# A state-space layer beside a gated feed-forward: state projection first, B transposed on TensorE, small angle tables, a fixed VectorE order

## The chip, the cores and the metric

The kernel runs on one core of a Trainium2 chip. The metric is the device time of one execution in microseconds. Before the change it is 227.94 us, the median of three runs (227.24, 227.94 and 227.97).

## The reference

The input x has 2048 rows of 512 numbers (bf16). Each row is normalised (xn). Two branches read xn:

- A diagonal state-space layer with 512 complex states: `h[t] = Lam_bar * h[t-1] + B_bar @ xn[t]`, with `Lam_bar = exp(dt * Lam)` and `B_bar = ((Lam_bar - 1) / Lam) * B`, and the output `s = 2 * Re(C @ h) + xn * Dskip`.
- A gated feed-forward of width 1376: `g = silu((gelu(xn @ w_gate) * (xn @ w_up)) @ w_down)`.

The result is `x + s * g`.

## The kernel before, in words

The 2048 rows are worked in four slabs (s = 0 to 3) of 512 rows. Columns of states and of the model are cut into tiles of 128: four for the states (pt), four for the model (kt), eleven for the feed-forward (j, the last with 96).

Per slab there are four kinds of TensorE work. `u_pair` (line 272) projects xn on the states, in two halves (h) of 16 matmuls; ScalarE evicts each group of four to `U`. `ffn` (324) makes one of eleven gate and up tiles (`g_ps`, `up_ps`); ScalarE evicts them as `gt` (with Gelu) and `ub`, and VectorE multiplies them to `at`. `down` (345) is 11 matmuls for 128 rows, four times a slab; ScalarE takes a Tanh of it and VectorE combines both to `g2`. `y_mm` (362) is the output projection of 128 rows from the states `hst` and the folded matrix `C2`; `epi` (378) multiplies with `g2`, adds x, and stores. PSUM has four buffers for `u_ps`, `g_ps` and `up_ps` together, two for `f_ps` and two for `y_ps`; `gt` and `ub` have four each.

`chain` (297) is the recurrence, on VectorE alone. The complex factor is split into its size `rho` and its angle: `rotate` (287) turns `U` by the tables of cosine and sine, real scans of 512 steps (four for a half of the states) run with `rho`, the last value is turned on for the next slab, and a second `rotate` gives `hst`. One half is 3.5 us of products, four scans, and 3.5 us of products.

Slab 0 has the order: eleven `ffn` tiles, with `fold_c` (254, C times the coefficients of B_bar, two ScalarE passes and two VectorE operations per state tile) after tiles 3 to 6; then the two state projections with their chains; then the norms of slabs 2 and 3; then `down`. Slabs 1 to 3 have the projections first, then the `ffn` tiles, and after tiles 4, 6, 8 and 10 an output projection of the slab before. The output projections of slab 3 come at the end.

What stands ahead of the loop: B and C are loaded by eight transposing DMAs each (lines 90 to 92 and 208 to 210); the weights are issued from ScalarE's queue, all else from SyncE's. `ln_stats` (132) and `ln_norm` (145) do the norms on VectorE, with the inverse root as a power on GpSimd; slab 0 is transposed on TensorE, the others by DMA (`ln_dma`, 153). The tables of 512 angles for four state tiles are made in full: VectorE multiplies and reduces the angles (lines 175 to 191), ScalarE takes the sine and the cosine (194, 195).

TensorE, ScalarE, SyncE and GpSimd run in the order written. VectorE does so only up to line 251; after it, a scheduler orders VectorE by priorities, with `at`, `g2` and the epilogue ahead of the chains (`tc.high_priority`).

Of the kernel before, what the change touches and what calls it, by code (L numbers as in the profile page):

```python
# [19 lines left out]
def kernel(  # L20
# [84 lines left out]
    halfpi = consts.tile([P, 1], FP32, name="halfpi")
    nc.vector.memset(halfpi[:], math.pi / 2)


    pt_ps = ps_y.tile([P, 16], BF16, name="pt_ps", tag="y")
    nc.tensor.transpose(pt_ps[:, :], pv[:, :], ident[0:16, 0:16])  # L110
    pf = consts.tile([P, 16], FP32, name="pf")
    nc.vector.tensor_copy(out=pf[:], in_=pt_ps[:, :])
    lre, lim, ldt, dsk = (pf[:, 4 * i : 4 * i + 4] for i in range(4))

    def small(name, w=NPT):
        return consts.tile([P, w], FP32, name=name)

    dt_ = small("dt_")
    nc.scalar.activation(out=dt_[:], in_=ldt, func=AF.Exp)
    a1 = small("a1")  # L120
    nc.vector.tensor_tensor(out=a1[:], in0=lre, in1=dt_[:], op=ALU.mult)
    thn = small("thn")
    nc.vector.scalar_tensor_tensor(
        out=thn[:], in0=lim, scalar=1.0 / (2.0 * math.pi), in1=dt_[:], op0=ALU.mult, op1=ALU.mult
    )
    rho = small("rho")
    nc.scalar.activation(out=rho[:], in_=a1[:], func=AF.Exp)


    xn_t = {}  # L130

    def ln_stats(s):
        st = work.tile([P, M, 6], FP32, name="st", tag="st")
        mv = consts.tile([P, M, 2], FP32, name=f"mv{s}")
        for m in range(M):
            nc.vector.bn_stats(out=st[:, m, :], in_=x_tok[:, s * M + m, :])  # L136
        for m in range(M):
            nc.vector.bn_aggr(out=mv[:, m, :], in_=st[:, m, :])
        ve = work.tile([P, M], FP32, name="ve", tag="ve")
        nc.vector.tensor_scalar(out=ve[:], in0=mv[:, :, 1], scalar1=EPS, scalar2=None, op0=ALU.add)  # L140
        rs = consts.tile([P, M], FP32, name=f"rs{s}")
        nc.gpsimd.tensor_tensor(out=rs[:], in0=ve[:], in1=mhalf[:], op=ALU.pow)  # L142
        return mv, rs

    def ln_norm(s, m, mv, rs):
        xn = work.tile([P, D], BF16, name="xn", tag="xn", bufs=4)
        nc.vector.tensor_scalar(  # L147
            out=xn[:], in0=x_tok[:, s * M + m, :], scalar1=mv[:, m, 0:1], scalar2=rs[:, m : m + 1],
            op0=ALU.subtract, op1=ALU.mult,
        )  # L150
        return xn

    def ln_dma(s):
        with tc.high_priority():
            mv, rs = ln_stats(s)
            xs = [ln_norm(s, m, mv, rs) for m in range(M)]
        for m in range(M):
            c0 = s * TS + m * P
            nc.sync.dma_start_transpose(out=xnT[:, :, c0 : c0 + P], in_=xs[m][:])

    mv, rs = ln_stats(0)
    xs = [ln_norm(0, m, mv, rs) for m in range(M)]
    for m in range(M):
        tp = ps_f.tile([P, KT, P], BF16, name="tp", tag="f")
        for kt in range(KT):
            nc.tensor.transpose(tp[:, kt, :], xs[m][:, kt * P : (kt + 1) * P], ident[:])  # L166
        nc.vector.tensor_copy(out=xnT[:, :, m * P : (m + 1) * P], in_=tp[:, :, :])


    cos_b = consts.tile([P, NPT, TS], BF16, name="cos_b")  # L170
    sinp = consts.tile([P, 2, NPT, TS], BF16, name="sinp")
    W2 = TS + 2
    ang = work.tile([P, NPT, W2], FP32, name="ang", tag="hst")
    angk = work.tile([P, NPT, W2], FP32, name="angk", tag="hst")
    for pt in range(NPT):
        nc.vector.tensor_scalar(
            out=ang[:, pt, :], in0=iota_f[:], scalar1=thn[:, pt : pt + 1], scalar2=None, op0=ALU.mult
        )
        nc.vector.tensor_scalar(
            out=angk[:, pt, :], in0=iota_f[:], scalar1=thn[:, pt : pt + 1], scalar2=MAGIC,  # L180
            op0=ALU.mult, op1=ALU.add,
        )

    nr = ang
    nc.vector.scalar_tensor_tensor(
        out=nr[:], in0=angk[:], scalar=MAGIC, in1=ang[:], op0=ALU.subtract, op1=ALU.subtract
    )
    ab = angk
    nc.vector.scalar_tensor_tensor(
        out=ab[:], in0=nr[:], scalar=-1.0, in1=nr[:], op0=ALU.mult, op1=ALU.max  # L190
    )
    cs = consts.tile([P, 2, NPT], FP32, name="cs")
    sn = consts.tile([P, 2, NPT], FP32, name="sn")
    nc.scalar.activation(out=sinp[:, 1, :, :], in_=nr[:, :, 0:TS], func=AF.Sin, scale=-TWO_PI)
    nc.scalar.activation(out=cos_b[:], in_=ab[:, :, 0:TS], func=AF.Sin, scale=-TWO_PI, bias=halfpi[:])
    for i, c in enumerate((1, TS)):
        nc.scalar.activation(out=sn[:, i, :], in_=nr[:, :, c], func=AF.Sin, scale=-TWO_PI)
        nc.scalar.activation(out=cs[:, i, :], in_=ab[:, :, c], func=AF.Sin, scale=-TWO_PI, bias=halfpi[:])
# [251 lines left out]
```

## Time and profile before

| | us |
|---|---|
| median of three runs | 227.94 |
| profiled execution | 225.93 |
| its span, first to last instruction | 224.2 |
| TensorE matmuls busy | 183.6 (82%) |
| VectorE busy | 173.4 (77%) |
| ScalarE busy | 95.1 (42%) |
| GpSimd busy | 6.4 (3%) |
| mean granted TensorE clock | 0.952 of full |

The profile is one execution. PE is TensorE, DVE VectorE, ACT ScalarE, POOL GpSimd, SP SyncE; a q behind a name is that engine's queue. L350 is line 350 of the kernel. Busy time counts instructions that overlap at their ends only once in a stretch, while the duration of one instruction is from its start to its end, so operations that follow each other start closer than they last.

### The profile page before, as it was taken

To read this page: it belongs to the slowest core of one execution; us is meant where nothing else is said; L and a number is where in the kernel's file an instruction comes from. 1 tells how busy PE (TensorE), PEld (TensorE's weight loads), DVE (VectorE), ACT (ScalarE), POOL (GpSimd) and SP (SyncE) were. 2 spreads that over 40 slices of the span, in tenths; PEclk is the share of its full clock that TensorE was granted. 3 is DMA by queue.
4 is the path that set the end of the run, shared out by engine and by line. 5 is a ranking of instruction groups with operands and counts; after the bars stand their busy time and mean duration, and the time that the engine had idled before them with its cause. 6 is when DMAs were issued, how large, how long until landed. Compare 5 with 4: busy or idle time off the path is not lost.

```text
span 224.2 us, 2436 instructions
## 1 busy us (share of the span) xinstructions
PE 183.6 (82%) x849; PEld 84.6 (38%) x865; DVE 173.4 (77%) x315; ACT 95.1 (42%) x156; POOL 6.4 (3%) x13
## 2 busy tenths in 40 slices
PE   0018939069966999999829999999999999999993
PEld 0013414024422444445303444444444444454441
DVE  1079869966899899999994279999932999995443
ACT  0221898177620466444201476444225764440310
POOL 3010000140000000000000000000000000000000
PEclk9999988769996999999967999999999999999998
DMA  6998992035510000000000000000100000001001
GB/s 189 327 230 176 341 183 60 0 50 97 107 32 0 0 3 0 0 1 23 26 23 23 0 0 3 0 23 0 47 26 1 0 0 0 26 24 49 23 5 68
DMA packets 24317, 12.26 MB, mean 55 GB/s; under 512 B 15760, under 2 KB 24304, under 8 KB 24304
## 3 DMA queue, kind: packets, MB, share of 16 engines
q1 hardware_dynamic: 21136, 9.28, 17.1%
q10 hardware_dynamic: 3168, 2.82, 4.8%
q8 instruction: 7, 0.11, 0.2%
q14 instruction: 6, 0.05, 0.1%
HBM read 6.33 MB, written 2.10 MB: 38 GB/s over the span
## 4 chain that ended last, share of the span: by engine, by line
PE 49%; DVE 36%; DMA 8%; ACT 4%; POOL 1%; issue 1%; SPq 0%; DVEq 0%; POOLq 0%
PE f_ps L350 13%; PE g_ps L330 10%; PE up_ps L335 9%; PE y_ps L367 9%; DVE Ft L306 8%; PE u_ps L280 6%; DVE st L136 4%; DVE pp L292 4%; DVE qq L293 4%; DMA xnT<-xn 4%; DVE at L343 3%; DMA wu<-in_B_w_up_dram 2%; DMA pv<-in_A_log_dt_dram 2%; DVE xn L147 2%; PE y_ps L372 1%; POOL rs L142 1%
## 5 line engine op out<-in xcount | busy, mean ns | idle before, releaser
L330 PE MATMUL g_ps<-xnT,wg 128*128 128x512 bf16 (+1 forms) x173 | 47.4, 396 | 8.1 <-ACT gt L339 7.4
L350 PE MATMUL f_ps<-wd,at 128*128 128x512 bf16 (+1 forms) x173 | 42.8, 405 | 8.9 <-DVE at L343 5.0
L335 PE MATMUL up_ps<-xnT,wu 128*128 128x512 bf16 (+1 forms) x174 | 46.8, 391 | 3.5 <-ACT ub L341 3.4
L339 ACT ACTIVATE gt<-g_ps 128x512 bf16<-128x512 f32 (+1 forms) x44 | 26.3, 597 | 33.8 <-PE g_ps L330 33.4
L341 ACT ACTIVATE ub<-up_ps 128x512 bf16<-128x512 f32 (+1 forms) x44 | 26.3, 598 | 11.8 <-PE up_ps L335 11.4
L354 ACT ACTIVATE th<-f_ps 128x512 f32<-128x512 f32 x16 | 9.6, 599 | 49.0 <-PE f_ps L350 41.7
L350 PEld LDWEIGHTS <-at 128*128 128x128 bf16 (+1 forms) x176 | 17.9, 103 | 32.3 <-issue 8.8
L367 PE MATMUL y_ps<-C,hst 128*128 128x512 bf16 x124 | 29.9, 379 | 0.2
L306 DVE TENSOR_TENSOR_SCAN Ft<-rho,it,Wt 128x512 bf16<-128x512 f32 x24 | 29.6, 1273 | 0.0
L330 PEld LDWEIGHTS <-wg 128*128 128x128 bf16 (+1 forms) x176 | 17.7, 103 | 28.3 <-issue 11.7
L280 PE MATMUL u_ps<-xnT,BT 128*128 128x512 bf16 x124 | 28.1, 379 | 0.2
L335 PEld LDWEIGHTS <-wu 128*128 128x128 bf16 (+1 forms) x176 | 18.2, 103 | 25.6 <-issue 6.5
L357 DVE SCALAR_TENSOR_TENSOR g<-th,f_ps 128x512 f32<-128x512 f32 x16 | 11.0, 686 | 19.1 <-ACT th L354 19.1
L284 ACT ACTIVATE U<-u_ps 128x512 bf16<-128x512 f32 x32 | 19.1, 598 | 8.2 <-PE u_ps L280 8.2
L280 PEld LDWEIGHTS <-BT 128*128 128x128 bf16 x128 | 12.5, 98 | 15.1
L343 DVE TENSOR_TENSOR at<-gt,ub 128x512 bf16<-128x512 bf16 (+1 forms) x44 | 18.0, 416 | 0.0
L367 PEld LDWEIGHTS <-hst 128*128 128x128 bf16 x128 | 12.4, 98 | 14.3
L292 DVE TENSOR_TENSOR pp<-U,cos_b 128x2048 bf16<-128x2048 bf16 x8 | 9.8, 1222 | 5.7 <-ACT U L284 5.5
L382 DVE TENSOR_TENSOR yg<-y_ps,g 128x512 bf16<-128x512 f32 x16 | 11.0, 686 | 2.3 <-PE y_ps L372 2.2
L166 PE MATMUL tp<-ident,xn 128*128 128x128 bf16 x16 | 2.0, 308 | 10.3 <-DVE xn L147 10.0
L147 DVE TENSOR_SCALAR xn<-x_tok,mv,rs 128x512 bf16<-128x512 bf16 x16 | 6.0, 411 | 5.5 <-DMA xnT<-xn 4.3
L136 DVE BATCH_NORM_STATS2 st<-x_tok 128x6 f32<-128x512 bf16 x16 | 10.1, 684 | 0.0
(74 smaller groups left out, 130.6 us busy)
## 6 DMA issues: line engine op xcount, KB each, us to landing
out_dram<-ot SPq DMA_DIRECT2D x16, 128.0 KB, 1.7
x_tok<-in_A_x_dram SPq DMA_DIRECT2D x3, 512.0 KB, 5.2
wd<-in_B_w_down_dram SPq DMA_DIRECT2D x1, 1280.0 KB
wg<-in_B_w_gate_dram ACTq DMA_DIRECT2D x1, 512.0 KB, 6.1
x_tok<-in_A_x_dram SPq DMA_DIRECT2D x4, 128.0 KB, 4.7
wu<-in_B_w_up_dram ACTq DMA_DIRECT2D x1, 512.0 KB
wg<-in_B_w_gate_dram ACTq DMA_DIRECT2D x1, 480.0 KB
wu<-in_B_w_up_dram ACTq DMA_DIRECT2D x1, 480.0 KB
```

What stands on the lines that cost most here:

```text
L136: nc.vector.bn_stats(out=st[:, m, :], in_=x_tok[:, s * M + m, :])
L280: nc.tensor.matmul(u_ps[:, :], lhsT=BT[:, ri, kt, pt * P : (pt + 1) * P], rhs=xnT[:, kt, cols], start=(kt == 0), stop=(kt == KT - 1),)
L284: nc.scalar.activation(out=U[:, ri, q, :], in_=u_ps[:, :], func=AF.Copy)
L292: nc.vector.tensor_tensor(out=pp[:], in0=src[:], in1=cb, op=ALU.mult)
L306: nc.vector.tensor_tensor_scan(out=Ft[:, ri, q, :], data0=rho[:, pt : pt + 1].to_broadcast([P, TS]), data1=Wt[:, ri, q, :], initial=init, ...
L330: nc.tensor.matmul(g_ps[:fs, :], lhsT=wg[:, kt, fsl], rhs=xnT[:, kt, cols], start=(kt == 0), stop=(kt == KT - 1))
L335: nc.tensor.matmul(u_ps[:fs, :], lhsT=wu[:, kt, fsl], rhs=xnT[:, kt, cols], start=(kt == 0), stop=(kt == KT - 1))
L339: nc.scalar.activation(out=gt[:fs], in_=g_ps[:fs, :], func=AF.Gelu_apprx_tanh)
L341: nc.scalar.activation(out=ub[:fs], in_=u_ps[:fs, :], func=AF.Copy)
L343: nc.vector.tensor_tensor(out=at[:fs, j, :], in0=gt[:fs], in1=ub[:fs], op=ALU.mult)
L350: nc.tensor.matmul(f_ps[:, :], lhsT=at[:fs, k, m0 : m0 + P], rhs=wd[:fs, k, :], start=(k == 0), stop=(k == NFT - 1))
L367: nc.tensor.matmul(y_ps[:, :], lhsT=hst[:, j // NPT, j % NPT, m0 : m0 + P], rhs=C2[:, j // NPT, j % NPT, :], start=(j == 0), stop=False,)
```

## The change

The state projection and the chains of slab 0 now come ahead of its `ffn` tiles. B is loaded as it lies and transposed by 32 matmuls. The angle tables are made by adding angles: sine and cosine of 49 columns (angles 0 to 31, and multiples of 32 up to 512), two broadcast copies on GpSimd, and six VectorE products and sums. The norms of slabs 2 and 3 are taken by ScalarE (two passes with a running sum, seven small GpSimd operations, a third ScalarE pass that normalises); slab 1 keeps its statistics on VectorE and is normalised on ScalarE. The inverse root of slab 0 is Exp(-0.5 Ln) on ScalarE. The weights and C move to SyncE's queue, `fold_c` to the down projections of slab 0, and C's tile shares the two buffers of `hst`. VectorE now runs in the order written, too; `later`, `dve`, `drain` and `flush` write it by two clocks that the code counts for itself.

```diff
-    for ri, src in enumerate((A_B_re, A_B_im)):
-        for kt in range(KT):
-            nc.sync.dma_start(out=BT[:, ri, kt, :], in_=src[:, kt * P : (kt + 1) * P], transpose=True)
+    for ri, src in enumerate((A_B_re, A_B_im)):
+        nc.scalar.dma_start(out=Bn[:, ri, :, :], in_=src.rearrange("(k p) d -> p k d", p=P))
...
+    ACT(out=tiny[:], in_=eps_t[:], func=AF.Ln)
+    def b_transposes(ri):
+        for k0 in range(0, KT, 2):
+            tb = ps_mm.tile([P, 2, D], BF16, name="tb_ps", tag="mm")
+            for k in range(2):
+                for pt in range(NPT):
+                    nc.tensor.transpose(
+                        tb[:, k, pt * P : (pt + 1) * P], Bn[:, ri, pt, (k0 + k) * P : (k0 + k + 1) * P], ident[:]
+                    )
+            ACT(out=BT[:, ri, k0 : k0 + 2, :], in_=tb[:, :, :], func=AF.Copy)
...
+    def rstd_act(s, a, b):
+        ACT(out=lnv[:, a:b], in_=mv[:, s, a:b, 1], func=AF.Ln, bias=eps_t[:])
+        ACT(out=rs[:, s, a:b], in_=lnv[:, a:b], func=AF.Exp, scale=-0.5)
...
+    dummies(6)
+    b_transposes(0)
...
+    rstd_act(0, 0, 2)
+    ACT(out=dt_[:], in_=ldt, func=AF.Exp)
+    b_transposes(1)
+    bn(0, 2)
...
+    rstd_act(0, 2, 4)
...
+    ACT(out=sb[:], in_=ang[:], func=AF.Sin, scale=TWO_PI)
+    ACT(out=cb[:], in_=kr[:], func=AF.Sin, scale=-TWO_PI, bias=halfpi[:])
+    nc.vector.tensor_copy(out=sh[:], in_=sb[:])
+    nc.vector.tensor_copy(out=ch[:], in_=cb[:])
+    nc.gpsimd.tensor_copy(out=v4(ca[:]), in_=ch[:, :, NB : NB + NA].unsqueeze(3).to_broadcast(W4))
+    nc.gpsimd.tensor_copy(out=v4(sa[:]), in_=sh[:, :, NB : NB + NA].unsqueeze(3).to_broadcast(W4))
...
+    def pe_takes(n, one=0.2157):
+        clk["pe"] += n * one
+    def pop():
+        r, c, f, _ = waiting.pop(0)
+        clk["dve"] = max(clk["dve"], r) + c
+        f()
+    def flush(key):
+        while any(w[3] == key for w in waiting):
+            pop()
+    def drain(t):
+        while waiting and max(clk["dve"], waiting[0][0]) + waiting[0][1] <= t + 1.0:
+            pop()
+    def dve(ready, cost, f):
+        drain(ready)
+        clk["dve"] = max(clk["dve"], ready) + cost
+        f()
+    def later(ready, cost, f, key=None):
+        waiting.append((ready, cost, f, key))
...
+        dve(now() + 0.9, 0.34, lambda: TT(out=at[:fs, j, :], in0=gt[:fs], in1=ub[:fs], op=ALU.mult))
...
+    def ln_act(s, m):
+        for i, f in enumerate((AF.Copy, AF.Square)):
+            junk = work.tile([P, D], BF16, name="junk", tag="junk", bufs=1)
+            ACT(out=junk[:], in_=x_tok[:, s * M + m, :], func=f, accum_out=sx[:, s, i, m : m + 1])
...
+    clk["pe"] = 10.0
+    clk["dve"] = 10.0
+    later(10.0, 1.2, lambda: TT(out=v4(t1_[:]), in0=v4(ca[:]), in1=cB, op=ALU.mult))
+    later(10.0, 1.2, lambda: TT(out=v4(t2_[:]), in0=v4(sa[:]), in1=sB, op=ALU.mult))
+    later(10.0, 1.2, lambda: TT(out=cos_b[:], in0=t1_[:], in1=t2_[:], op=ALU.subtract))
...
+    for h in range(2):
+        chain(0, h, u_pair(0, h), hst0)
...
+    dve(17.0, 2.8, ln1_stats)
...
+        for j in range(NFT):
+            ffn(s, j, ats[s])
+            if s == 0:
+                if j == 1:
+                    dve(now(), 2.6, coefficients)
+                if 3 <= j < 3 + M:
+                    ln_out(1, j - 3)
+            else:
+                if s < NS - 1:
+                    if j < M:
+                        ln_act(s + 1, j)
+                    if j == M:
+                        ln_small(s + 1)
+                    if 6 <= j < 6 + M:
+                        ln_out(s + 1, j - 6)
...
         if s < NS - 1:
             for m in range(M):
                 g2s[s, m] = down(s, m, ats[s])
+                if s == 0:
+                    fold_c(m)
```

`chain` and `rotate` hand their operations to `later`, `y_mm` calls `flush` for the states that it reads, and `ln_out` is a ScalarE pass with scale and shift and a transposing DMA.

## Rows read from the trace of the kernel before

**Rows 1.** Busy time by stretch: length, then each engine's busy us, clock, DMA, GB/s

```profile
0.00:18.60 18.60, 2.21 (x17) 1.83 (x18) 6.71 (x23) 2.98 (x4) 2.90 (x10) 1.00 1.01 247
18.65:22.60 3.95, 3.95 (x12) 1.47 (x12) 3.92 (x9) 1.20 (x2) 0.00 (x0) 1.00 0.64 160
60.30:75.40 15.10, 11.31 (x45) 4.73 (x45) 14.37 (x20) 2.40 (x4) 0.00 (x0) 0.89 0.11 21
82.30:116.70 34.40, 29.33 (x144) 13.72 (x145) 34.16 (x57) 13.75 (x23) 0.00 (x0) 0.96 0.04 12
126.00:169.20 43.20, 42.99 (x210) 20.23 (x213) 34.64 (x55) 20.33 (x34) 0.00 (x0) 1.00 0.04 13
169.20:220.30 51.10, 50.84 (x256) 24.23 (x259) 38.08 (x54) 20.94 (x35) 0.00 (x0) 1.00 0.05 16
```

**Rows 2.** Waits from 0 to 60 us: total us, times, longest

```profile
PE g_ps L330 <- ACT gt L339: 7.4, 3, 6.3
PE up_ps L335 <- ACT ub L341: 3.4, 1, 3.4
```

**Rows 3.** Waits from 60 to 117 us

```profile
PE f_ps L350 <- DVE at L343: 5.0, 2, 4.1
PE f_ps L350 <- DVE g L357: 3.7, 1, 3.7
```

**Rows 4.** The chain of waits that ended last: start, length, what

```profile
57.70 0.66 DVE C L259
...
60.01 1.14 DVE pp L292
...
63.60 4.49 DVE Ft L306 x4
...
159.81 9.51 PE f_ps L350 x44
...
176.23 0.86 PE g_ps L330 x4
...
220.38 0.70 DVE yg L382
```

**Rows 5.** All engines in order of time, 0 to 62 us

```profile
15.36 1.38 DVE L147 TENSOR_SCALAR xn<-x_tok,mv,rs 128x512 bf16<-128x512 bf16 x4 [1.22 <-POOL rs L142]
15.82 1.04 PE L166 MATMUL tp<-ident,xn 128*128 128x128 bf16 x8 [10.04 <-DVE xn L147]
...
18.65 1.87 PE L330 MATMUL g_ps<-xnT,wg 128*128 128x512 bf16 x4 [0.51 <-DVE xnT L167]
...
21.77 1.03 PE L330 MATMUL g_ps<-xnT,wg 128*128 128x512 bf16 x4
```

**Rows 6.** ScalarE in order of time, 30 to 36 us

```profile
30.19 0.19 ACT L197 ACTIVATE sn<-ang 128x4 f32<-128x4 f32 x1
...
33.15 0.59 ACT L341 ACTIVATE ub<-up_ps 128x512 bf16<-128x512 f32 x1
33.62 0.72 ACT L257 ACTIVATE tA<-CT,cim 128x512 f32<-128x512 bf16 x1
34.24 0.72 ACT L258 ACTIVATE tB<-CT,cim 128x512 f32<-128x512 bf16 x1
```

**Rows 7.** ScalarE in order of time, 9 to 32 us: start, length, what

```profile
11.45 1.28 ACT L339 ACT_TABLE_LOAD   x1
20.55 0.60 ACT L339 ACTIVATE gt<-g_ps 128x512 bf16<-128x512 f32 x1 [7.82 <-PE g_ps L330]
26.47 1.91 ACT L194 ACTIVATE sinp<-ang 128x2048 bf16<-128x2048 f32 x1
```

**Rows 8.** GpSimd's groups by form: busy us, mean ns of one, idle before

```profile
L142 POOL TENSOR_TENSOR rs<-ve,mhalf 128x4 f32<-128x4 f32 x4 | 4.6, 1157 | 40.3 <-DVE ve L140 40.3
L100 POOL CAST iota_f<-iota_i 128x514 f32<-128x514 int32 x1 | 0.6, 614 | 0.1
...
masks.py:199 POOL TENSOR_SCALAR_AFFINE_SELECT ident_f<-ident_f 128x128 f32<-128x128 f32 x1 | 0.3, 293 | 0.1
...
L102 POOL MEMSET mhalf<- 128x4 f32 x1 | 0.1, 102 | 0.0
```

More of the change, by code (lines that the diff above doesn't have):

```diff
@@ L44 @@
     NPT = 4
+    H2 = NPT // 2
     TS = 512
@@ L105 @@
[L105 to L198, printed above, removed]
@@ L207 @@
     nc.sync.dma_start(out=wd[:FL, NFT - 1, :], in_=B_w_down[(NFT - 1) * P : F, :])
[L208 to L216 removed]
+    warm = consts.tile([P, TS], BF16, name="warm")
+    nc.vector.memset(warm[:], 0.0)
+    halfpi = consts.tile([P, 1], FP32, name="halfpi")
@@ new lines, with small, dummies @@
+    iota_f = consts.tile([P, NBA], FP32, name="iota_f")
+    nc.gpsimd.tensor_copy(out=iota_f[:], in_=iota_i[:])
+    mhalf = consts.tile([P, M], FP32, name="mhalf")
+    nc.gpsimd.memset(mhalf[:], -0.5)
+    tiny = consts.tile([P, 1], FP32, name="tiny")
+    ACT(out=tiny[:], in_=eps_t[:], func=AF.Ln)
+    def small(name, w=NPT):
+        return consts.tile([P, w], FP32, name=name)
+    def dummies(n):
+        w_ps = ps_f.tile([P, TS], FP32, name="w_ps", tag="f")
+        for _ in range(n):
+            nc.tensor.matmul(w_ps[:, :], lhsT=warm[:, 0:P], rhs=warm[:], start=True, stop=True)
@@ new lines @@
+    rho = small("rho")
+    ACT(out=rho[:], in_=a1[:], func=AF.Exp)
+    for m in range(2, 4):
+        tp = t_xn0(m, xs[m])
+        nc.vector.tensor_copy(out=xnT[:, :, m * P : (m + 1) * P], in_=tp[:, :, :])
+    W3 = [P, NPT, NBA]
+    ang = consts.tile(W3, FP32, name="ang")
+    kr = consts.tile(W3, FP32, name="kr")
+    sb = consts.tile(W3, FP32, name="sb")
+    cb = consts.tile(W3, FP32, name="cb")
+    sh = consts.tile(W3, BF16, name="sh")
+    ch = consts.tile(W3, BF16, name="ch")
+    TT(out=ang[:], in0=iota_f[:].unsqueeze(1).to_broadcast(W3), in1=thn[:].unsqueeze(2).to_broadcast(W3), op=ALU.mult)
@@ L297, in chain, with wt, wt_dst @@
     def chain(s, h, U, hst):
         hs = slice(h * H2, (h + 1) * H2)
-        Wt = work.tile([P, 2, H2, TS], BF16, name="Wt", tag="Wt")
-        rotate(Wt[:, 0, :, :], Wt[:, 1, :, :], U, h, ALU.add)
-        Ft = work.tile([P, 2, H2, TS], BF16, name="Ft", tag="Ft")
+        ready = now() + 0.9
+        box = {}
+        def wt():
+            box["W"] = work.tile([P, 2, H2, TS], BF16, name="Wt", tag="Wt", bufs=1)
+            return [box["W"][:, i, :, :] for i in range(2)]
+        def wt_dst():
+            return wt() if "W" not in box else [box["W"][:, i, :, :] for i in range(2)]
@@ L324, in ffn @@
+        if s < NS - 1:
+            later(ready, 0.5, carry)
+        rotate(
+            lambda: [hst[:, i, hs, :] for i in range(2)], lambda: box["F"], h, (ALU.subtract, ALU.add), ready,
+            ("h", s, h),
+        )
     def ffn(s, j, at):
```

335 lines of the change are left out of this document (217 added, 118 removed).

## The prediction

> **What bounds the kernel now.** I read the table by stretch first: it shows where TensorE loses time. From 126.0 us on it loses nothing: the 43.2 us up to 169.2 hold 42.99 us of matmuls at a granted clock of 1.00, and VectorE is busy for 34.64 of them, so it has 8.6 us to spare in a slab [rows 1]. That stretch is one whole slab: state projection, eleven gate/up pairs with four output projections between them, four down projections. The last slab carries four more output projections and takes 51.1 us [rows 1], so four are 7.9; slab 0 has none. The program's matmuls thus need 35.3 + 43.2 + 43.2 + 51.1 = 172.8 us at the full clock.
>
> The first gate matmul starts at 18.65 us, the last matmul ends near 220.3 [rows 1], and 3.9 us of VectorE work and store follow to 224.2. Between 18.65 and 126.0 lie 107.3 us; slabs 0 and 1 need 78.5 of them, so 28.8 us are lost there and almost none later. The waits name the losers: up to 60 us the gate matmuls stand 7.4 us behind ScalarE's evictions and the up matmuls 3.4 us, because ScalarE makes the full tables and folds C in the middle of slab 0 [rows 2]; from 60 to 117 us the down projection waits 5.0 us for `at` and 3.7 us for `g2`, both on VectorE [rows 3], which is busy for 34.16 of the 34.40 us before 116.7 [rows 1]. VectorE gets the first chain only at 60.01 [rows 4], since slab 0 projects the state last. So the early slabs are bound by the start and by VectorE, the late ones by TensorE.
>
> **The change, part by part.** I call T the time at which the first projection of slab 0 can start, add TensorE's 172.8 us, then what it loses, then the tail.
>
> *T.* B no longer goes through eight transposing DMAs, but must be in SBUF whole, be transposed by 32 small matmuls and evicted in four pieces. Ahead of or beside its second half go x of slab 0 and the first weights, 2.25 MB together; at the 247 GB/s of the first 18.6 us [rows 1] that is there at 9.1 us. Eight transposes take 1.04 us [rows 5], so the first eviction may begin at 10.2. ScalarE has by then evicted the first half and computes the first row norms as Ln and Exp, 0.2 us each (0.19 for four columns [rows 6]). An eviction of 1024 columns lies between 0.60 for 512 and 1.91 for 2048 [rows 7]: 1.05. Then Ln and Exp for tiles 2 and 3, two normalisations on VectorE (four take 1.38 [rows 5]: 0.74), four transposes (0.52), a copy (0.4). The unknown is table loads: a load of 1.28 us stands ahead of the first Gelu although that one's data come 7.82 us later [rows 7], and in this kernel every new function but Copy and Tanh has one. The order is Ln, Exp, Ln, Exp, Sin, Gelu, and no row has Ln. Between no load and three more (3.85 us) I take three, since the rows that there are show a load at each switch. All three lie on the path: 11.3 for the second half's first eviction, 13.4 after both, 16.4 for the norms, T = 18.5. Without them T = 14.65.
>
> The Trainium skill says otherwise: "ScalarE: Activation LUTs", section "Table sets: the hidden batching unit", has Ln and Exp in one named set, so one load. No run here shows it; by that rule T would be the smaller one.
>
> *The tables and VectorE's order in slab 0.* Everything that VectorE does is now in an order written by the code's own two clocks, both at 10 when the projection starts, with the table operations taken as ready at that moment. They are not. After T come four operations on 196 columns and two sines (2.5 us with their hand-overs), two casts (0.5), then two GpSimd copies of 2048 columns. GpSimd's rows give 0.29 us for 128 columns and 0.61 for 514 [rows 8]: 1.9 by that slope, 2.45 in proportion; 64 separate runs at the 0.10 of the smallest row would be 6.4. I take 2.2, since the cast is the nearest row. So the second copy lands at T+7.4; the first table product (1.14 us, as the 2048-column products [rows 4]) hides beside it, and VectorE runs 6.3 us behind its own plan. What it has before `at` of the last tile of slab 0: by the code's clocks `at` is due at 36.8 and takes everything that fits before 37.8. That is six table operations (7.2), statistics of slab 1 (2.8), coefficients (2.6), eleven `at` (3.7), and 11.3 us of the first half's chain: 27.6 in all. With 6.3 us of lateness and 0.9 for hand-overs `at` comes at T+34.8. TensorE wants it at 6.9 (projection, 169.32 to 176.23) + 11 x 1.73 (two groups of 0.86 [rows 4]) + 2.2 (ten matmuls of the first down projection) = T+28.1. Loss 6.7. In it is the low clock at the start: from 18.65 to 21.77 eight matmuls took 3.1 us instead of 1.7, so at 1.2 GHz, though the view prints 1.00 for that stretch; only sixteen transposes lay before [rows 1, 5]. That costs nothing beyond the 6.7, for VectorE is later than both. The same lateness shows earlier as ScalarE waiting at the normalisation of slab 1, which is part of it.
>
> The Trainium skill, "SBUF — State Buffer", section "Who interferes with whom", says that a VectorE operation with two SBUF inputs and a GpSimd operation that reads SBUF exclude each other. By that rule the first product would not hide beside the second copy, 1.1 us more. The rows of before hold only four-column GpSimd operations beside VectorE, so no run here shows it yet.
>
> *Behind that, slabs 0 and 1.* The folds of C go between the down projections (eight operations of 0.66), the chain's second half follows. VectorE finishes slab 0's state at T+57; TensorE wants it at T+34.8 + 7.3 + 6.9 + 8.6 = T+57.6. That just fits (7.3 for the three down projections left, of 9.51 for four [rows 4], 8.6 for five tiles). But slab 1's chain starts ten us late and only 8.6 us are spare in a slab, so at the third down projection of slab 1 the balance is short again: 81 us of VectorE work and waits against 80 wanted. I take 2.0 us for both this and the lower clock after the broken down projections of slab 0 (before, the stretch around them had a clock of 0.89 [rows 1]); the two cover each other, so one sum. Bounds 0 and 4.
>
> *Norms on ScalarE.* In slabs 1 and 2 each of the first four tiles has two evictions (0.48 apart) and two passes over x (0.62 apart [rows 6]), 2.2 us against TensorE's 1.73; four PSUM buffers take up most of it. I take 0.5 a slab, 1.0; if a pass costs 0.8, 2.5 in all. It frees VectorE of 12 normalisations and 8 statistics (about 9 us). The seven small GpSimd operations between (0.10 to 1.16 each [rows 8], 0.7 to 8) have 5.4 us of TensorE work as cover; at the top they would cost 2.7 a slab, at the likely 2.5 us nothing.
>
> *End.* The last chain is no longer cut short by priorities: in the code's clocks its last combination stands behind the last `at`, about 1.1 us after TensorE asks for it. Tail 3.9 as before. SyncE's weights and B now share the start, but the 6.1 MB up to the down weights take 25 us at 247 GB/s, and the first down projection is at T+26; the C transposes and the transposes of slab 1 follow on SyncE and are wanted at T+37 and later. Nothing.
>
> **Sum.** 18.5 + 172.8 + (6.7 + 2.0 + 1.0 + 1.1) + 3.9 = 206.0 span; 1.7 lies around the span in the profiled execution (225.93 to 224.2), so 207.7. The three runs of before lie 1.3 to 2.0 above their profiled one; with 1.5 I forecast 209.2.
>
> **Rivals.**
> - *One load for Ln and Exp.* T falls by 3.85: 205.4. Ln and Exp would find their tables together, as Gelu and Tanh do here; against it: Exp, Gelu and Sin each had a load. The Trainium skill's section on table sets, above, states it.
> - *GpSimd's broadcasts are slow.* They come one after the other and VectorE waits for both, so each further us per copy costs two. At 6.4 us per copy the time is 217.6. For it: 64 short runs; against it: the cast at 1.2 ns a column.
> - *Slower than before, by the same place.* The table operations head the fixed order, `at` stands behind them, and TensorE and ScalarE stop when four `gt` tiles are full. From 11.7 us per copy (9.5 more than taken, twice) the time passes 228; at 12 us it is 228.8. For it: a GpSimd power on four columns takes 1.16 us, 0.29 a column [rows 8], 45 times what is needed; against it: the cast.
> - *The change doesn't do what it says.* `hst` of slab 1 shares two buffers with slab 0's and with C. If it gets slab 0's, its first write stands in VectorE's order before `at` of the last two tiles but must wait for the last output projection of slab 0, some 5 us of VectorE, and slab 1 has none to spare: 214. Against it: C's buffer is free earlier.
>
> **Chances.** Forecast 0.45, one load 0.29, slow broadcasts 0.10, shared buffer 0.08, slower 0.05, no gain 0.03. The range goes from one load with the cheap ends of the other terms (205.4 - 2 for the balance, - 1 for the norms, - 0.6 for the copies = 202) to the slow broadcasts (218). A measurement here tells 0.3% (0.7 us) from nothing; faster 0.92, same 0.02, slower 0.06.
>
> **What would show it.** T: the first projection at 18.5 with six table loads, or at 14.7 with three. GpSimd's two copies at 2.2 us. `at` of slab 0's last tile near T+35, the down projection waiting there 5 to 7 us in sum. From slab 2 on TensorE over 98% busy at 1.00. If VectorE still paces slabs 2 and 3, or the projection of slab 0 waits for B's copy, the argument is wrong.

## The result, and the profile after

The changed kernel takes 205.53 us, the median of four runs (205.40 to 207.09), beside 227.68 for the kernel before on the same chip: a ratio of 0.9045, with an interval of 0.8997 to 0.9092. On a second chip it was 206.86 (205.21 to 206.91) beside 227.08 (0.9067, 0.9009 to 0.9126); experiment 11 shows the one stretch that makes the difference. The forecast was 209.2. The profiled execution took 205.63 us, of which 203.5 are span. In experiment 9 one execution of four, the profiled one, was held back (487.13 us), so its time there is that of the other three and only the first 101.88 us of its trace are read.

First the page of the profile of the changed kernel: the busy time of each engine, and the rows of the 40 slices for TensorE, VectorE, ScalarE and the granted clock.

```profile
PE 184.6 (91%) x903; PEld 86.6 (43%) x903; DVE 166.4 (82%) x283; ACT 114.5 (56%) x207; POOL 14.2 (7%) x31
...
PE   5617999996999999999599999999799999999992
...
DVE  1427799999999898999999988999419999994443
ACT  2695486892777897751147997751256644441210
...
PEclk9975799999999999999999999999999999999999
```

TensorE's busy time is that of before (183.6), in a span 20.7 us shorter. Of its row three dents are left behind the start: at slices 10, 20 and 29, each at the end of one of the slabs 0 to 2.

Then the table by stretch of the changed kernel, cut where slabs 0 to 3 start their state projections, within 0.2 us (length, busy time of PE, PEld, DVE, ACT, POOL, clock, DMA share, GB/s). It answers to [rows 1].

```profile
0.00:17.67 17.67, 8.21 (x55) 5.18 (x56) 6.65 (x23) 11.46 (x16) 1.48 (x11) 0.86 0.94 298
17.67:58.76 41.09, 38.61 (x165) 16.83 (x165) 38.39 (x78) 26.92 (x46) 6.34 (x6) 0.94 0.38 91
58.76:104.24 45.48, 43.37 (x214) 20.27 (x212) 43.27 (x68) 28.04 (x56) 3.19 (x7) 1.00 0.09 23
104.24:148.66 44.42, 43.37 (x214) 20.25 (x212) 38.75 (x61) 27.15 (x54) 3.19 (x7) 1.00 0.10 25
148.66:199.70 51.04, 51.02 (x261) 24.12 (x258) 38.24 (x54) 20.89 (x35) 0.00 (x0) 1.00 0.05 16
```

The slabs need 35.3, 43.2, 43.2 and 51.1 us of TensorE; they took 41.1, 45.5, 44.4 and 51.0. So 9.2 us are lost, where the kernel before lost 28.8. TensorE's waits from 17.67 to 200 us tell where (total us, times, longest); the 0.5 for `xnT` lies just ahead of the projection:

```profile
PE f_ps L438 <- DVE g L445: 3.2, 2, 2.1
PE f_ps L438 <- DVE at L431: 2.3, 2, 1.8
PE u_ps L336 <- DVE xnT L211: 0.5, 1, 0.5
PE g_ps L418 <- ACT gt L428: 0.2, 1, 0.2
```

The 10.8 us behind ScalarE's evictions [rows 2] are gone but for 0.2, and the 8.7 us of the down projection behind `at` and `g2` [rows 3] have become 5.5. The wait on `at` is in slab 0, the two on `g` (the code's `g2`) at the third down projection of slabs 1 and 2. Most of the rest of slab 0's loss, 2.5 us, is its projection, which took 9.44 us instead of 6.9, at a mean granted clock of 0.73, so partly at 1.2 and partly at 2.4 GHz; ahead of it lay 1.2 us of transposes, and ahead of these a wait of 4.3 us for the norms.

Now ScalarE ahead of the projection, in order of time (start, length, what). It answers to [rows 7].

```profile
8.56 0.30 ACT L159 ACTIVATE lnv<-mv,eps_t 128x2 f32<-128x2 f32 x1
8.88 1.28 ACT L160 ACT_TABLE_LOAD   x1
10.17 0.20 ACT L160 ACTIVATE rs<-lnv 128x2 f32<-128x2 f32 x1
...
10.37 1.92 ACT L145 ACTIVATE BT<-tb_ps 128x1024 bf16<-128x1024 bf16 x2
12.31 1.28 ACT L159 ACT_TABLE_LOAD   x1
13.61 0.30 ACT L159 ACTIVATE lnv<-mv,eps_t 128x2 f32<-128x2 f32 x1
13.92 1.28 ACT L160 ACT_TABLE_LOAD   x1
15.21 0.20 ACT L160 ACTIVATE rs<-lnv 128x2 f32<-128x2 f32 x1
```

Each change between Ln and Exp has a load: with a first Ln load at 1.82 us they are four, three more than one load for both would be. And the broadcast copies on GpSimd, for which [rows 8] gave the estimate, with VectorE's first table products beside them (two views):

```profile
19.83 1.89 POOL L240 COPY ca<-ch 128x2048 bf16<-128x2048 bf16 x1 [17.61 <-DVE ch L228]
21.66 1.90 POOL L241 COPY sa<-sh 128x2048 bf16<-128x2048 bf16 x1
```

```profile
21.75 2.91 DVE L519 TENSOR_TENSOR t__248<-ca,ch 128x2048 bf16<-128x2048 bf16 x1 [1.99 <-POOL ca L240]
24.59 1.25 DVE L520 TENSOR_TENSOR t__249<-sa,sh 128x2048 bf16<-128x2048 bf16 x1
```

The first product lies beside the second copy, takes 2.91 us where its twin takes 1.25, and ends 1.1 us after the copy.

### The profile page after: what moved, and what is told of

It is laid out like the page before. It is cut to its first block, busy times and chain, and to the rows that moved or that the text cites. A ratio compares the mean times of both kernels' runs of the same rounds, so it can differ in the third digit from the quotient of the medians.

```text
span 203.5 us, 2555 instructions
## 1 busy us (share of the span) xinstructions
PE 184.6 (91%) x903; PEld 86.6 (43%) x903; DVE 166.4 (82%) x283; ACT 114.5 (56%) x207; POOL 14.2 (7%) x31
## 3 DMA queue, kind: packets, MB, share of 16 engines
q10 hardware_dynamic: 1056, 1.05, 1.6%
## 4 chain that ended last, share of the span: by engine, by line
PE 43%; DVE 36%; ACT 14%; DMA 2%; issue 2%; POOL 1%; ACTq 0%
PE f_ps L438 13%; PE u_ps L336 10%; DVE Ft L382 7%; PE y_ps L457 7%; PE up_ps L423 6%; PE g_ps L418 6%; ACT junk L489 5%; DVE at L431 4%; DVE pp L352 3%; DVE qq L352 3%; DVE yg L475 3%; ACT ub L430 3%; DMA Bn<-in_A_B_re_dram 2%; DVE hst L356 2%; DVE Wt L356 2%
## 5 line engine op out<-in xcount | busy, mean ns | idle before, releaser
L418 PE MATMUL g_ps<-xnT,wg 128*128 128x512 bf16 (+1 forms) x176 | 45.2, 379 | 0.2 <-ACT gt L428 0.2
L423 PE MATMUL up_ps<-xnT,wu 128*128 128x512 bf16 (+1 forms) x176 | 45.2, 379 | 0.0
L438 PE MATMUL f_ps<-wd,at 128*128 128x512 bf16 (+1 forms) x176 | 39.4, 379 | 5.5 <-DVE g L445 3.2
L336 PE MATMUL u_ps<-xnT,BT 128*128 128x512 bf16 x128 | 30.8, 403 | 0.5 <-DVE xnT L211 0.5
L382 DVE TENSOR_TENSOR_SCAN Ft<-rho,it,Wt 128x512 bf16<-128x512 f32 x24 | 30.4, 1275 | 0.0
L438 PEld LDWEIGHTS <-at 128*128 128x128 bf16 (+1 forms) x176 | 17.0, 98 | 26.4 <-issue 3.7
L336 PEld LDWEIGHTS <-BT 128*128 128x128 bf16 x128 | 13.2, 103 | 17.5 <-issue 3.8
L445 DVE SCALAR_TENSOR_TENSOR g<-th,f_ps 128x512 f32<-128x512 f32 x16 | 10.8, 679 | 11.0 <-ACT th L443 11.0
L356 DVE TENSOR_TENSOR hst<-pp,qq 128x1024 bf16<-128x1024 bf16 x16 | 10.6, 686 | 0.2
L356 DVE TENSOR_TENSOR Wt<-pp,qq 128x1024 bf16<-128x1024 bf16 x16 | 10.6, 685 | 0.1
L504 ACT ACTIVATE xn<-x_tok,nb,rs 128x512 bf16<-128x512 bf16 x12 | 9.7, 809 | 1.6 <-POOL nb L537 1.6
```

The costliest lines, as they stand in the source:

```text
L336: nc.tensor.matmul(u_ps[:, :], lhsT=BT[:, ri, kt, pt * P : (pt + 1) * P], rhs=xnT[:, kt, cols], start=(kt == 0), stop=(kt == KT - 1),)
L356: return lambda: TT(out=dst()[i], in0=box["pp"][:, i, :, :], in1=box["qq"][:, 1 - i, :, :], op=op)
L382: nc.vector.tensor_tensor_scan(out=box["F"][:, ri, q, :], data0=rho[:, pt : pt + 1].to_broadcast([P, TS]), data1=box["W"][:, ri, q, :], in ...
L418: nc.tensor.matmul(g_ps[:fs, :], lhsT=wg[:, kt, fsl], rhs=xnT[:, kt, cols], start=(kt == 0), stop=(kt == KT - 1))
L423: nc.tensor.matmul(u_ps[:fs, :], lhsT=wu[:, kt, fsl], rhs=xnT[:, kt, cols], start=(kt == 0), stop=(kt == KT - 1))
L438: nc.tensor.matmul(f_ps[:, :], lhsT=at[:fs, k, m0 : m0 + P], rhs=wd[:fs, k, :], start=(k == 0), stop=(k == NFT - 1))
```

## The experiments

Each kernel is the changed one with the edit shown, cut at "...". Times are medians; the difference is to 205.5 us, or, for the last four, to the 206.9 of the changed kernel measured beside them. Experiments 4 and 6 to 8 ran on that second chip too: beside 206.9 their times are 1.3 us better than said. Single executions of the changed kernel differ by up to 1.7 us (experiment 11), so where a difference is small, traces are compared and not medians alone.

**1. No Ln in the norms of slab 0.** Tests the three loads.

```diff
-    ACT(out=tiny[:], in_=eps_t[:], func=AF.Ln)
+    ACT(out=tiny[:], in_=eps_t[:], func=AF.Exp)
...
-        ACT(out=lnv[:, a:b], in_=mv[:, s, a:b, 1], func=AF.Ln, bias=eps_t[:])
-        ACT(out=rs[:, s, a:b], in_=lnv[:, a:b], func=AF.Exp, scale=-0.5)
+        TSC(out=lnv[:, a:b], in0=mv[:, s, a:b, 1], scalar1=EPS, scalar2=None, op0=ALU.add)
+        nc.gpsimd.tensor_tensor(out=rs[:, s, a:b], in0=lnv[:, a:b], in1=mhalf[:, a:b], op=ALU.pow)
```

> The inverse root of slab 0 is taken as a power on GpSimd again, so ScalarE has three table loads instead of six. Theory (the start is set by ScalarE's loads): the first projection starts near 13.3 us instead of 17.7, all behind it keeps its distance, and the time falls by 4.4 us to about 201. Rival (the start is set by B or by the weights, or the later waits grow by what the start gives): start at 16 or later, or time above 204.

Measured 202.46 us (0.8923, 0.8877 to 0.8969). The projection starts at 13.56 instead of 17.67, 4.1 us earlier, about three loads of 1.28. The median fell by 3.1 only. TensorE waits for `at` as long as before (2.3 us), since VectorE's lateness moves with T; and behind that wait it ran the rest of slab 0's down projections at a mean clock of 0.81, so partly at 1.2 GHz, 1.6 us longer than in the trace above. The row of that stretch, by the columns of the table above:

```profile
47.20:56.17 8.97, 8.92 (x34) 3.69 (x36) 7.64 (x11) 5.45 (x9) 0.00 (x0) 0.81 0.01 2
```

That stretch isn't a price of the edit: the changed kernel shows it too in its other trace (experiment 11). Beside that trace the projection starts 3.7 us earlier (13.56 and 17.30) and the span is 3.7 us shorter (201.0 and 204.7), so the start's gain came through whole.

**2. Each broadcast copy twice.** Tests that the copies pace VectorE.

```diff
+    for _ in range(2):
         nc.gpsimd.tensor_copy(out=v4(ca[:]), ...)
+    for _ in range(2):
         nc.gpsimd.tensor_copy(out=v4(sa[:]), ...)
```

> Each of GpSimd's two broadcast copies (1.9 us) is done twice. Theory (VectorE's lateness in slab 0 goes straight to the end, because VectorE paces until slab 2): the first table product starts 3.8 us later, the time rises by 3.5 to 4 us to about 209.3. Rival (the copies are off the path, buffers and slack of slabs 1 and 2 take them up): below 207.

Measured 208.72 us (0.9216, 0.9174 to 0.9258), 3.2 slower. VectorE's second product starts at 27.86 instead of 24.59, 3.3 later, and nearly all of it comes to TensorE: a gate matmul waits 5.4 us for `gt`, in place of 0.2 there and 2.3 for `at`. So the lateness of the tables is the loss in slab 0 behind its projection. The first product again takes 2.91, now beside the two copies of `sa`; these take 4.75 us together where the two of `ca` take 3.84, so the copies are held up as well.

**3. The second copy on ScalarE.** Tests the exclusion of VectorE and GpSimd.

```diff
-    nc.gpsimd.tensor_copy(out=v4(sa[:]), ...)
+    ACT(out=v4(sa[:]), ..., func=AF.Copy)
```

> The second broadcast copy goes from GpSimd to ScalarE, so that no GpSimd operation runs beside the first table product. Theory (the product's 2.91 us are a wait for GpSimd's copy): the product takes 1.2 us, VectorE gains 1.7 us, the time falls by 1.2 to 1.7 us to about 204. Rival (the product is slow by its operands, inner runs of 32): it still takes 2.9 us and the time stays, or rises because ScalarE's evictions start 1.9 us later.

Measured 204.89 us (0.9016, 0.8971 to 0.9061). VectorE, in order of time, with the copy on ScalarE in the same microseconds:

```profile
21.38 1.26 DVE L519 TENSOR_TENSOR t__248<-ca,ch 128x2048 bf16<-128x2048 bf16 x1 [1.99 <-POOL ca L240]
22.55 1.25 DVE L520 TENSOR_TENSOR t__249<-sa,sh 128x2048 bf16<-128x2048 bf16 x1
```

The product now takes 1.26, and slab 1 starts 2.0 us earlier (56.59 instead of 58.60), of which 0.4 is an earlier projection (17.30). Slab 1 gave 1.7 back: the wait for `g` stayed at 2.1, and from 90 to 103.73 the mean clock was 0.88 (in the changed kernel the slab's is 1.00). So the product is shown to be 1.65 us shorter and slab 0 1.6 us; the median, 0.6 lower, is within the spread of the changed kernel.

**4. ScalarE's passes spread.** One pass over x per tile on tiles 0 to 7, not two on tiles 0 to 3; the normalisations two by two at tiles 9 and 10.

```diff
-    def ln_act(s, m):
-        for i, f in enumerate((AF.Copy, AF.Square)):
+    def ln_act(s, m, k):
+        for i, f in ((0, AF.Copy), (1, AF.Square))[k : k + 1]:
...
-                    if j < M:
-                        ln_act(s + 1, j)
-                    if j == M:
+                    if j < 2 * M:
+                        ln_act(s + 1, j // 2, j % 2)
+                    if j == 2 * M - 1:
                         ln_small(s + 1)
-                    if 6 <= j < 6 + M:
-                        ln_out(s + 1, j - 6)
+                    if j >= NFT - 2:
+                        ln_out(s + 1, 2 * (j - NFT + 2))
+                        ln_out(s + 1, 2 * (j - NFT + 2) + 1)
```

> ScalarE's eight passes for the sums of the next slab are spread over the first eight tiles, one each, instead of two each over the first four. Theory (ScalarE, 2.3 us a tile there against TensorE's 1.73, brings at late, VectorE idles 3.4 us for it, and that comes back as the waits of 2.1 and 1.05 us for g2 in the down projections of slabs 1 and 2): those waits fall to about 0.5 in sum, the time falls by 2 to 3 us to about 203. Rival (VectorE is short of time in slab 1 whatever ScalarE does): within 0.7 us of 205.5.

Measured 202.09 us (0.8886, 0.8842 to 0.8929), 3.4 faster; in the traces slabs 1 and 2 together are 3.1 shorter. First ScalarE over one tile of slab 1 in the changed kernel, and VectorE's `at` there (two views):

```profile
69.30 0.58 ACT L428 ACTIVATE gt<-g_ps 128x512 bf16<-128x512 f32 x1
69.78 0.59 ACT L430 ACTIVATE ub<-up_ps 128x512 bf16<-128x512 f32 x1
70.26 0.63 ACT L489 ACTIVATE junk<-x_tok 128x512 bf16<-128x512 bf16 x1
70.78 0.20 ACT L489 ACTIVATION_READ_ACCUMULATOR junk<-x_tok 128x1 f32 x1
71.01 0.63 ACT L489 ACTIVATE junk<-x_tok 128x512 bf16<-128x512 bf16 x1
71.55 0.19 ACT L489 ACTIVATION_READ_ACCUMULATOR junk<-x_tok 128x1 f32 x1
71.64 0.58 ACT L428 ACTIVATE gt<-g_ps 128x512 bf16<-128x512 f32 x1
```

```profile
70.40 0.42 DVE L431 TENSOR_TENSOR at<-gt,ub 128x512 bf16<-128x512 bf16 x1 [0.78 <-ACT ub L430]
```

With the passes spread, slabs 1 and 2 by stretch:

```profile
58.18:101.80 43.62, 43.37 (x214) 20.29 (x213) 43.15 (x68) 27.99 (x56) 3.40 (x7) 1.00 0.10 24
101.80:145.01 43.21, 43.21 (x214) 20.28 (x212) 38.67 (x62) 27.10 (x54) 3.94 (x7) 1.00 0.10 25
```

VectorE is as busy as before (43.15 us beside 43.27), and the waits for `g` are 0.2 us in sum instead of 2.1 and 1.05. So the balance of VectorE was not what failed in slabs 1 and 2: the passes delayed `ub`, VectorE stood still for it (1.9 us in slab 1, now 0.2), and what it lost there the third down projection paid. The edit also moves the third passes, from tiles 6 to 9 to the last two; but VectorE's three waits for `ub` stand ahead of the `at` at 70.40, 75.07 and 77.41, where the first two passes run.

**5. VectorE's code clock six later.** `clk["dve"]` starts at 16 instead of 10, so less of the chain goes ahead of `at` in slab 0.

```diff
-    clk["dve"] = 10.0
+    clk["dve"] = 16.0
```

> The code's own VectorE clock starts at 16 instead of 10, as late as VectorE really is, so at stands ahead of more of the first chain; the work is the same. Theory (VectorE's work is the limit until slab 2): the wait of 2.6 us at the first down projection of slab 0 goes, and as much comes back at the output projections of slab 0 or in slab 1; the time stays within 1 us of 205.5. Rival (the order alone is at fault): about 203.

Measured 208.54 us (0.9204, 0.9164 to 0.9243): 3.0 slower, where the theory had 1 either way. The wait of slab 0 did go, and slab 1 starts at 54.25 instead of 58.60. But the first output projection then waits for the states that were put off (TensorE in order of time):

```profile
54.25 7.07 PE L336 MATMUL u_ps<-xnT,BT 128*128 128x512 bf16 x32
76.93 2.74 PE L457 MATMUL y_ps<-C,hst 128*128 128x512 bf16 x6 [6.55 <-DVE hst L356]
```

**6. VectorE by the scheduler's priorities.** The fixed order is dropped.

```diff
-        tc.manual_schedule(engines={ENG.PE, ENG.Activation, ENG.SP, ENG.Pool, ENG.DVE})
+        tc.manual_schedule(engines={ENG.PE, ENG.Activation, ENG.SP, ENG.Pool})
```

> One part undone: VectorE is again ordered by the scheduler's own priorities, with the operations written in the same order; the other engines keep theirs. Theory (VectorE's work, not its order, is the limit until slab 2): within 3 us of 205.5. Rival (the fixed order is a main source of the gain): 212 or more.

Measured 210.80 us (0.9266, 0.9215 to 0.9318), 5.3 slower. The projection starts at 21.65, 4 us later: in the new order VectorE stands for 6.2 us, up to 13.64, at a statistics operation whose x has not landed. Behind the start `at` costs 5.5 us instead of 2.3, `g` 1.2 instead of 3.2. So the fixed order is worth 4 to 5 us (3.9 beside 206.9), between the two theories, and most of it lies ahead of the projection.

**7. The projection of slab 0 after its feed-forward tiles.**

```diff
-    for h in range(2):
-        chain(0, h, u_pair(0, h), hst0)
...
+        if s == 0:
+            for h in range(2):
+                chain(0, h, u_pair(0, h), hst0)
```

> One part undone: in slab 0 the state projection and its chain come after the eleven gate and up tiles again; the rest as in the changed kernel. Theory (VectorE could not begin the chain before about T+16 anyway, as its tables, statistics and coefficients fill that time): the loss is small, the time rises by 1.5 to 4 us to about 208. Rival (the early projection is the main source of the gain): 213 or more.

Measured 219.74 us (0.9664, 0.9600 to 0.9728), 14 slower (12.9 beside 206.9): my own theory here (1.5 to 4) fell. Two waits carry it, this one on TensorE and its cause on ScalarE, from two views:

```profile
36.42 1.87 PE L418 MATMUL g_ps<-xnT,wg 128*128 128x512 bf16 x4 [7.31 <-ACT gt L428]
```

```profile
35.08 0.81 ACT L504 ACTIVATE xn<-x_tok,nb,rs 128x512 bf16<-128x512 bf16 x1 [8.78 <-POOL nb L535]
```

The normalisation of slab 1 stands in ScalarE's order at tile 3 and needs statistics that VectorE takes behind the tables; without 9 us of projection ahead of the tiles nothing covers that. The other wait is 7.8 us of the first output projection for `hst`. So the early projection serves twice: it gives VectorE its chain, and it covers the tables.

**8. Norms of slabs 2 and 3 on VectorE, pulled in as a whole.** The four normalisations stand in the list behind the chain, and a `flush` after tile 8 writes everything up to them.

```diff
-                    if j < M:
-                        ln_act(s + 1, j)
                     if j == M:
-                        ln_small(s + 1)
-                    if 6 <= j < 6 + M:
-                        ln_out(s + 1, j - 6)
+                        ln_vec(s + 1)
+                    if j == 8:
+                        flush(("n", s + 1))
```

> One part undone: the norms of slabs 2 and 3 go back to VectorE (4.2 us a slab, inserted at the fifth tile), ScalarE is free of them. Theory (VectorE paces through slab 1 and has 4 us to spare in slab 2, ScalarE costs 3 us there): plus 1 to 3 us, about 207.5. Rival (ScalarE's passes are the dearer place): below 205. Rival (VectorE has the room): no change.

Measured 230.38 us (1.0123, 1.0057 to 1.0190), 25 slower (23.5 beside 206.9), far from every theory. TensorE stood 13.47 us once in slab 1 and 8.93 once in slab 2; VectorE shows why in slab 1, in order of time:

```profile
95.28 4.80 DVE L382 TENSOR_TENSOR_SCAN Ft<-rho,it,Wt 128x512 bf16<-128x512 f32 x4
...
104.14 1.37 DVE L504 TENSOR_SCALAR xn<-x_tok,mv,rs 128x512 bf16<-128x512 bf16 x4
...
106.49 0.75 DVE L431 TENSOR_TENSOR at<-gt,ub 128x512 bf16<-128x512 bf16 x2
```

From 87.9 us VectorE works without a gap through the second half of the chain and the normalisations, and the last two `at` come behind all of it. That was the order that I wrote, not the work on VectorE, as the next experiment shows.

**9. The same norms on VectorE, each operation where it is due.** Statistics after tile 4, one normalisation after each of the tiles 7 to 10.

```diff
+    def norm_vec(s, m):
...
+        dve(now() - 0.9, 0.34, lambda: TSC(
...
-                    if j < M:
-                        ln_act(s + 1, j)
                     if j == M:
-                        ln_small(s + 1)
-                    if 6 <= j < 6 + M:
-                        ln_out(s + 1, j - 6)
+                        ln_vec(s + 1)
+                    if 7 <= j < 7 + M:
+                        norm_vec(s + 1, j - 7)
```

> The norms of slabs 2 and 3 back on VectorE, but this time each operation put into the written order one by one where the code's clocks have it due (statistics after tile 4, one normalisation after each of the tiles 7 to 10), so that nothing of the chain is pulled ahead of an at. Theory A: what counts is VectorE's load: 4.2 us more a slab (2.46 + 0.36 + 1.38), 43.3 + 4.2 = 47.5 us in slab 1 where the slab takes 45.5, and 38.8 + 4.2 = 43.0 in slab 2, which just fits: 2 to 4 us slower than the changed kernel, 207.5 to 209.5 us, and the ScalarE waits of at (3.4 us in sum) fall away. Theory B: any VectorE norm in these slabs upsets the order as in the first trial (25 us): over 215 us.

Measured 202.73 us (0.8904, 0.8848 to 0.8960): 4.1 faster than the changed kernel's median on the same chip and 2.5 faster than its fastest execution there (205.21, at a mean clock of 1.00), against both theories. Slab 1:

```profile
58.39:101.88 43.49, 43.16 (x210) 20.24 (x213) 42.98 (x75) 21.18 (x36) 1.27 (x2) 1.00 0.10 25
```

With the norms on it VectorE still fits, and TensorE runs through; VectorE waits 0.2 us for `ub` in place of 1.9. Moving these norms to ScalarE, as the change does it, therefore cost time. It need not: spread as in experiment 4, the program took 202.09.

**10. B through transposing DMAs again,** issued from SyncE, the weights from ScalarE.

```diff
-    for ri, src in enumerate((A_B_re, A_B_im)):
-        nc.scalar.dma_start(out=Bn[:, ri, :, :], in_=src.rearrange("(k p) d -> p k d", p=P))
...
+    for ri, src in enumerate((A_B_re, A_B_im)):
+        for kt in range(KT):
+            nc.sync.dma_start(out=BT[:, ri, kt, :], in_=src[:, kt * P : (kt + 1) * P], transpose=True)
...
-        nc.sync.dma_start(out=wg[:, :, a:b], in_=wg_r[:, :, a:b])
-        nc.sync.dma_start(out=wu[:, :, a:b], in_=wu_r[:, :, a:b])
+        nc.scalar.dma_start(out=wg[:, :, a:b], in_=wg_r[:, :, a:b])
+        nc.scalar.dma_start(out=wu[:, :, a:b], in_=wu_r[:, :, a:b])
...
-    b_transposes(0)
...
-    b_transposes(1)
```

> B again through eight transposing DMAs, issued from SyncE right behind x and the parameters, the weights issued from ScalarE; no transposes of B on TensorE, no evictions. Theory A: the eight issues take 12.3 us of SyncE (1.54 each before), the last starts at about 15 us and lands 3 us later, so the projection starts at 18.5 to 20 instead of 17.7 and the kernel is 1 to 3 us slower: 206.5 to 208.5 us; B on TensorE was a small part of the gain. Theory B: the start is bound by the chain of norms and table loads alone (xnT complete at 17.2), B's transposes lie beside it in either form: 205.5 us, within 0.7. Theory C: the transposing DMAs and the weights slow each other, as the 8.1 us from issue to landing of the first four before hint: T over 22 us, 210 us or more.

Measured 212.33 us (0.9349, 0.9278 to 0.9419), 5.5 slower, with the projection at 22.42. The time is that of theory C. ScalarE in order of time:

```profile
7.09 0.42 ACTq L99 DMA_DIRECT2D wg<-in_B_w_gate_dram  x1
13.32 0.39 ACTq L100 DMA_DIRECT2D wu<-in_B_w_up_dram  x1
13.74 1.28 ACT L127 ACT_TABLE_LOAD   x1 [13.74 <-DMA BT<-in_A_B_re_dram]
...
15.15 0.28 ACT L160 ACTIVATE lnv<-mv,eps_t 128x2 f32<-128x2 f32 x1
```

ScalarE issues its last weight only at 13.32, and the first Ln runs at 15.15 instead of 8.56. In the changed kernel the same six issues on SyncE lie between 5.64 and 10.68, so it is not their number that takes so long here. The two edits went together, so what B's transposes alone are worth stays open, and so does what held up the issues; what is shown is that the weights' issues on ScalarE, beside B's transposing DMAs, hold up the new start.

**11. The changed kernel again,** beside runs 9, 10 and 12.

> The changed kernel once more, on the chip on which the next three run, so that they can be compared with it directly. Both theories: 205.5 us (205.4 to 207.1 in the runs so far), slab 0's projection starts at 17.1 to 17.7 us.

206.86 us, as in the result above, with four executions at 205.21, 206.86, 206.87 and 206.91. The profiled one is 1.2 us above that of the result, and one stretch holds it: TensorE's matmuls from the second wait for `at` in slab 0 to the projection of slab 1. Here and in the first trace:

```profile
50.87:59.86 8.99, 8.94 (x34) 3.73 (x35) 7.62 (x11) 5.45 (x9) 0.00 (x0) 0.81 0.01 2
```

```profile
51.24:58.60 7.36, 7.36 (x34) 3.33 (x35) 7.33 (x11) 5.45 (x9) 0.00 (x0) 1.00 0.01 2
```

The same work takes 1.6 us more at a mean clock of 0.81, behind the same wait of 1.80 us; the rest of the slabs agrees, and the start is 0.4 earlier here.

**12. Edits 1, 3 and 4 together.**

> Three edits together: no Ln in slab 0's norms (three table loads fewer), the second broadcast copy on ScalarE, and ScalarE's passes over x spread over eight tiles. Theory A: each takes away another wait (start of the projection, the at of slab 0's last tile, the g of the third down projection), so the gains of the single runs add: 205.5 - 3.1 - 0.6 - 3.4 = 198.4 us (197.5 to 199.5), with no wait of a down projection over 1 us. Theory B: all three meet the same VectorE, which is what paces slabs 0 and 1, and what one edit frees the next cannot free again: no better than 200.5 us, with VectorE busy for over 95% of slab 1.

Measured 196.93 us (0.8650, 0.8603 to 0.8696), 9.9 less than the changed kernel's median beside it and 8.3 less than its fastest execution there. Theory A holds and is exceeded, since two of its terms were too small: by traces with the same clock the parts are 3.7 (experiment 1), 1.6 (slab 0 in experiment 3) and 3.1 (experiment 4), 8.4 in sum. By stretch:

```profile
0.00:13.52 13.52, 8.84 (x55) 5.71 (x56) 6.69 (x25) 6.90 (x9) 2.98 (x13) 1.00 0.87 283
13.52:52.80 39.28, 36.67 (x160) 16.46 (x164) 36.58 (x78) 28.27 (x47) 4.50 (x5) 1.00 0.56 132
52.80:96.42 43.62, 43.16 (x210) 20.28 (x212) 43.14 (x68) 27.98 (x56) 3.39 (x7) 1.00 0.10 24
96.42:139.63 43.21, 42.99 (x209) 20.25 (x212) 38.66 (x62) 27.09 (x54) 3.93 (x7) 1.00 0.10 25
```

Slabs 1 to 3 run at TensorE's rate. Slab 0 still loses 4.0 us (39.28 - 35.3): 2.2 in the waits for `at`, and 1.2 in the projection, 8.1 us instead of 6.9.

## Why the prediction was right, step by step

*T.* Forecast 18.5, measured 17.67 in the profiled execution and 16.8 to 17.5 in other traces of the same start. The disputed term, three extra loads, is as forecast: the loads are there (1.28 us each), and without them T is 13.56 (experiment 1). B was put too late: its second half was there by 8.08, when its transposes start, and not at 9.1, as the first 17.67 us moved 298 GB/s and not 247; ScalarE's own order paced the start. And the terms that are named come to 18.1, not 18.5 (16.4 + 0.74 + 0.52 + 0.4). The rival with one load had the right total (205.4) for the wrong reason; its T of 14.65 did not come. The Trainium skill, "ScalarE: Activation LUTs", section "Table sets: the hidden batching unit", lists a set that holds both Ln and Exp; this program loads a table at every change between the two, and here the measurement decides.

*Tables and slab 0.* Copies forecast at 2.2 us took 1.9. The first product was forecast to hide beside the second copy and did not: 2.91 us instead of 1.25, and 1.26 once the copy was on ScalarE. The Trainium skill, "SBUF — State Buffer", section "Who interferes with whom", says that a VectorE operation with two SBUF inputs and a GpSimd operation that reads SBUF exclude each other; the traces agree. The two misses are 0.6 less and 1.7 more. `at` of the last tile came at T+33.5 beside T+34.8; TensorE's losses in the slab were 5.8 beside 6.7. Their place was not as forecast: the sign named, 5 to 7 us of waiting at the down projection, did not show. It waited 2.3, and 2.5 went to the low clock in the projection, which the forecast had at 1.4 and within the 6.7.

*Slabs 1 and 2.* Balance and low clock 2.0 and norms 1.0, together 3.0; measured 2.3 + 1.2 = 3.5. The place was right, the third down projection, and the sum is near, but that is luck: the cause was wrong. I had VectorE ten us late and the passes nearly hidden by four PSUM buffers. Experiments 4 and 9 show the reverse: VectorE's load fits even with the norms on it, and ScalarE's passes are the cause. A pass takes 0.62, but each has a read of its running sum of 0.19 us behind it that I did not count, so a tile needs 2.33 us of ScalarE where TensorE gives 1.73. "It frees VectorE of about 9 us" was true and worth little: with the norms on VectorE (9) the program took 202.73, with the passes spread (4) 202.09. With these waits slab 2 was 97.6% busy on TensorE (43.37 of 44.42), just under the 98% that was named as a sign.

*End.* Forecast 1.1, measured nothing: TensorE is busy for 51.02 of the last slab's 51.04 us. VectorE's last combination ends at 183.42, within the projection that reads it (it starts at 182.20).

*The other rivals.* Slow broadcasts did not come (1.9 us a copy); what that rival calls 45 times is about 50 (0.29 us a column beside 11.7 us for 2048). The shared buffer cost nothing: no wait of VectorE for a buffer of `hst` stands in the profile.

*Outside the span.* The largest single miss of the sum. I added 1.5 us because the runs of before lay that far above their profiled execution; here the profiled one (205.63) and the median (205.53) agree. By the sum against the profiled execution I was 2.1 high (207.7): 0.8 in T, 0.9 in slab 0, 1.2 at the end and 0.1 in the tail too much, 0.5 in slabs 1 and 2 and 0.4 around the span too little.

*Not settled.* Why the clock falls behind a wait of about 2 us in some executions and not in others: behind the wait for `at` in slab 0 the changed kernel ran at 1.00 in one profiled execution and at 0.81 in the other, and after the wait for `g` in slab 1 at 1.00, experiment 3 at 0.88. Norms on VectorE (9) with edits 1 and 3 was not run.

## What to carry to other kernels

When work is moved off a busy engine, look at what the engine that takes it holds in its order: two short passes between evictions stopped VectorE's input, and spreading the same passes over twice as many tiles gave about 3 us with the same load. In an order fixed by hand, a late start of one operation moves everything behind it: doubling the copies cost 3.2 us of 3.3, and writing one list out too early cost 25. Add up one profiled execution, and do not carry the offset of one kernel's runs over to another's. When an edit gains less or more than its trace explains, look first whether one stretch of the two traces ran at different clocks: here one such stretch was worth 1.6 us.

## What the runs showed of the hardware that was not expected

- A change between Ln and Exp costs a load of 1.28 us each way in this program; an inverse root as VectorE add and GpSimd power (0.73 to 0.79 us for two columns) avoids it and starts the projection 3.7 to 4.1 us earlier.
- A ScalarE pass with a running sum is followed by an instruction of 0.19 us that reads the sum; two such passes and two evictions fill 2.33 us.
- A VectorE product of 2048 columns took 2.91 us beside a GpSimd copy and 1.26 beside the same copy on ScalarE; two such copies beside it took 4.75 us where two alone took 3.84. The copy takes 1.89 us on either engine.
- A queue of weight loads on ScalarE, with transposing DMAs on SyncE beside it, kept its first function until 13.74 us, though the functions' data were there earlier (statistics at 5.6).
- Behind the same wait of 1.80 us the same 34 matmuls took 7.36 us in one execution, at a clock of 1.00, and 8.99 in another, at 0.81.
